# Attention and token mix moved into the second half of each MLP pass, with scores in threes and a new PSUM layout

## Chip, cores and metric

The kernel runs on one core of one Trainium2 chip. The metric is the time of one execution on the device, in microseconds (us); lower is better. Each kernel ran several times, beside the kernel before on the same chip.

## The reference, cut to what matters

Eight batches go through grouped-query attention (16 query heads, 4 key heads, 384 tokens, head size 64) and then through a ResMLP layer of width 1024.

```python
def reference(q, k, v, alpha1, beta1, w_tok, alpha2, beta2, w_ch1, w_ch2, lam):
    x = attention(q, k, v)                     # per batch [384, 1024], softmax over the keys
    a1 = alpha1 * x + beta1
    tok = einsum('ts,bsd->btd', w_tok, a1)     # token mix
    u = x + lam * tok
    a2 = alpha2 * u + beta2
    ch = maximum(a2 @ w_ch1, 0) @ w_ch2        # the MLP: 1024 -> 4096 -> 1024
    return u + lam * ch
```

## The kernel before

It makes eight passes, numbered 0 to 7. Pass b runs the MLP of batch b on TensorE (`main`), and between its matmuls the attention and token mix of batch b+1 (`side`). A pass has two halves. The first computes hT with 256 matmuls of 384 columns (group h) and streams the first weight matrix, 16 blocks of 512 KB, through a ring of five buffers. The second computes the output with 192 matmuls of 512 columns (group ch) from resident weights, so nothing streams then except the first five blocks of the next pass.

```python
RING = 5
def load_w1(n):                                   # one block of the first weights, cast on the way
    t = sb.tile([P, NDT, CW * P], bf, tag="w1", name="w1", bufs=RING)
    nc.gpsimd.dma_start(out=t, in_=w1src[...])
def flip_k(b):                                    # k and q of batch b, transposed by DMA, on SyncE's queue
    nc.sync.dma_start_transpose(out=kT..., in_=k2s[b]...)     # 1,536 packets of 256 B
def flip_q(b):
    nc.sync.dma_start_transpose(out=qT..., in_=qrs[b]...)     # 3,072 packets of 256 B
# ... cut: loads, transposes, constants ...
def main(b):
    for c in range(NCH):                          # first half: 16 blocks of weights
        w1 = w1_tiles.pop(b * NCH + c)
        for j in range(CW):
            ps = psum.tile([P, 512], f32, tag="mm", name="h", bufs=2)
            for dt in range(NDT):
                nc.tensor.matmul(out=ps[:, :n], lhsT=w1[...], rhs=a2T[...], ...)
            # ... relu to hT on ACT or VectorE, in turn ...
        load_w1(b * NCH + c + RING)
    for dw in range(NDW):                         # second half
        for ms in range(NST):
            ...                                   # 32 ch matmuls, two VectorE operations, output store
# the main loop of before: pieces of side() spread evenly over the pass
    for dt in main(b):
        t += dt
        if done < len(us) and done * t_all * span < len(us) * (t - t_all * lead):
            us[done](); done += 1
        if not loaded and t > t_all * 0.55:
            load_next(b + 2)
        if not flipped and t > t_all * (0.85 if b else 0.75):
            flip_k(b + 2); flip_q(b + 2)
```

In `side`, scores come two groups at a time (`scores2`); a group is a PSUM tile of two banks, exponentiated by ACT. Then come av (attention times v; VectorE divides and scales), tok (token mix; VectorE adds and scales) and a2T (transposed by DMA for the next pass).

The softmax here doesn't subtract the row's maximum and nothing guards it: scores larger than these inputs give would overflow.

## Time and profile before

| | before |
|---|---|
| median | 811.8 us (811.3 to 812.1, 3 runs) |
| TensorE busy in the profile | 98% of 808.8 us |
| a steady pass (2 to 6) | 97.45 us |
| its first / second half | 48.85 / 48.6 us |
| last pass, first half, no attention in it | 41.6 us |

A profile line of a group gives source line, engine, operation, output<-inputs, count, then busy time and mean length of one, then the engine's idle time ahead of it and what ended most of it. A timeline line gives start, length, engine and group. The busy time by stretch, here for the two halves of the pass that starts at 331 us, gives for each stretch its length, each engine's busy time with instruction count, the granted clock, the DMA share and GB/s:

```profile
331.00:379.85 48.85, 48.75 (x396) 29.51 (x395) 19.97 (x37) 19.27 (x27) 13.16 (x15) 1.00 1.31 167
379.85:428.44 48.59, 48.11 (x336) 24.58 (x342) 21.29 (x39) 7.04 (x8) 7.90 (x12) 1.00 0.66 108
```

TensorE is full in both halves, and the DMA moves 167 GB/s in the first and 108 in the second. The issues of SyncE's queue show the k and q transposes late in that second half:

```profile
415.50 1.46 SPq L113 DMA_TRANSPOSE kT<-k  x1
417.14 3.94 SPq L117 DMA_TRANSPOSE qT<-q_raw  x1
```

Their issue takes 5.6 us in all.

### The profile page before, as it was taken

Reading aid. Unit: us, or ns where it says so; the run is one execution under the profiler, and the core shown is the slowest. Engines: PE = TensorE matmul, PEld = TensorE weight load, DVE = VectorE, ACT = ScalarE, POOL = GpSimd, SP = SyncE. Lnnn points to the kernel's source line nnn. Section 1 sums busy time; section 2 is a strip of 40 time slices with the busy share of each in tenths; the row PEclk is TensorE's granted clock in tenths of the full one; section 3 lists DMA queues with packets and bytes.
Section 4 is the critical chain, followed back from the end, with each engine's and each line's share of the span. In section 5 each row is a group of like instructions: output and inputs, shape, how many; then the busy total and the mean of one; then the engine's idle time right before and its main releaser. Section 6 shows DMA issues by size and latency. Waiting matters only on the chain.

```text
span 808.8 us, 14107 instructions
## 1 busy us (share of the span) xinstructions
PE 795.7 (98%) x6076; PEld 450.2 (56%) x6129; DVE 343.3 (42%) x669; ACT 226.0 (28%) x311; POOL 178.4 (22%) x232
## 2 busy tenths in 40 slices
PE   8999999999999999999999999999999999999997
PEld 4766554665556645565455654556555565556545
DVE  7645452344433444344452445434444244432122
ACT  6654212332123311233103331034211332102100
POOL 7234320324003230124102250022400320003000
PEclk9999999999999999999999999999999999999999
DMA  9999999999279993799748996499935999129511
GB/s 192 198 207 200 207 197 185 172 178 148 54 139 181 171 133 80 130 178 175 100 113 128 173 180 88 100 154 166 184 60 113 151 171 126 40 66 190 81 40 40
DMA packets 233550, 112.96 MB, mean 140 GB/s; under 512 B 82952, under 2 KB 227344, under 8 KB 233488
## 3 DMA queue, kind: packets, MB, share of 16 engines
q0 software_dynamic: 170736, 83.47, 83.9%
q1 hardware_dynamic: 62208, 28.20, 14.8%
q8 instruction: 48, 0.79, 0.4%
q10 hardware_dynamic: 544, 0.39, 0.2%
q14 instruction: 14, 0.11, 0.0%
HBM read 170.53 MB, written 12.58 MB: 226 GB/s over the span
## 4 chain that ended last, share of the span: by engine, by line
PE 92%; DVE 4%; DMA 3%; issue 1%; ACT 0%; POOL 0%; SPq 0%; DVEq 0%
PE h L413 39%; PE ch L448 38%; PE av L237 4%; PE sc L202 4%; PE tok L259 4%; DMA w<-in_moe_w_ch_dram 2%; DVE x L243 1%; DVE hT L423 1%; PE h L152 1%; DVE a1f L250 0%; DMA a2T<-a 0%; DVE a L252 0%; PE warm L466 0%; PE ut L276 0%; PE tp L188 0%
## 5 line engine op out<-in xcount | busy, mean ns | idle before, releaser
L413 PE MATMUL h<-a2T,w 128*128 128x384 bf16 (+1 forms) x2016 | 349.7, 326 | 1.0 <-DVE hT L423 0.3
L448 PE MATMUL ch<-w,hT 128*128 128x512 bf16 (+2 forms) x1547 | 345.3, 370 | 4.3 <-issue 1.0
L413 PEld LDWEIGHTS <-w 128*128 128x128 bf16 x2016 | 189.4, 98 | 125.8 <-issue 9.0
L448 PEld LDWEIGHTS <-hT 128*128 128x128 bf16 x1600 | 146.3, 98 | 154.2 <-issue 5.8
L128 POOL DMA_DIRECT2D w<-in_moe_w_ch_dram x128 | 112.6, 882 | 540.9 <-PE h L413 502.1
L211 ACT ACTIVATE es<-sc 128x1024 bf16<-128x1024 f32 x126 | 123.4, 1021 | 289.8 <-PE sc L202 289.8
L423 DVE TENSOR_SCALAR hT<-h,bias 128x384 bf16<-128x384 f32 x128 | 79.0, 618 | 187.9 <-PE h L413 187.4
L421 ACT ACTIVATE hT<-h,bias 128x384 bf16<-128x384 f32 x128 | 74.3, 581 | 203.1 <-PE h L413 202.6
L453 DVE TENSOR_TENSOR o<-ch,vecs 128x512 f32<-128x512 f32 (+2 forms) x50 | 33.4, 667 | 91.1 <-PE ch L448 91.1
L266 DVE TENSOR_TENSOR x<-tok,x 128x384 f32<-128x384 f32 x64 | 35.6, 556 | 80.2 <-PE tok L259 78.0
L237 PEld LDWEIGHTS <-es 128*128 128x128 bf16 x1008 | 45.8, 97 | 20.5
L237 PE MATMUL av<-v,es 128*128 128x65 bf16 x1008 | 49.0, 193 | 0.0
L202 PE MATMUL sc<-qT,kT 64*128 64x384 bf16 (+2 forms) x576 | 45.5, 272 | 0.7 <-DMA qT<-q_raw 0.6
L259 PEld LDWEIGHTS <-wtokT 128*128 128x128 bf16 x576 | 37.8, 98 | 13.8 <-DVE x L243 1.6
L242 DVE RECIPROCAL rinv<-av 128x6 f32<-128x6 f32 x64 | 12.4, 193 | 71.2 <-PE av L237 70.9
L259 PE MATMUL tok<-a,wtokT 128*128 128x128 bf16 x504 | 37.3, 219 | 0.0
L243 DVE TENSOR_TENSOR x<-av,rinv 128x384 f32<-128x384 f32 x64 | 35.7, 557 | 2.2
L202 PEld LDWEIGHTS <-kT 64*128 64x128 bf16 x576 | 20.2, 94 | 28.4 <-issue 23.9
L454 DVE TENSOR_TENSOR o<-o,x 128x512 f32<-128x512 f32 (+2 forms) x50 | 33.6, 671 | 1.7
L270 DVE TENSOR_TENSOR a<-x,vecs 128x384 bf16<-128x384 f32 x56 | 31.7, 566 | 1.9
L250 DVE TENSOR_TENSOR a1f<-x,vecs 128x384 f32<-128x384 f32 x56 | 31.5, 562 | 1.9
L252 DVE TENSOR_TENSOR a<-a1f,vecs 128x384 bf16<-128x384 f32 x56 | 31.2, 558 | 2.2
(75 smaller groups left out, 194.7 us busy)
## 6 DMA issues: line engine op xcount, KB each, us to landing
w<-in_moe_w_ch_dram POOLq DMA_DIRECT2D x138, 512.0 KB, 7.8
out_dram<-o SPq DMA_DIRECT2D x47, 256.0 KB, 2.2
q_raw<-in_q_dram POOLq DMA_DIRECT2D x28, 192.0 KB, 7.2
kst<-in_k_dram SPq DMA_DIRECT2D x16, 192.0 KB, 3.2
w<-in_moe_w_ch_dram POOLq DMA_DIRECT2D x1, 2048.0 KB, 16.2
v<-in_v_dram POOLq DMA_DIRECT2D x24, 64.0 KB, 7.0
w<-in_moe_w_ch_dram POOLq DMA_DIRECT2D x4, 256.0 KB, 10.0
a2T<-a SPq DMA_TRANSPOSE x54, 2.3
```

What stands on the lines that cost most here:

```text
L128: nc.gpsimd.dma_start(out=t, in_=w1src[:, :, c * CW * P:(c + 1) * CW * P])
L202: nc.tensor.matmul(out=sc[:, hh, k % 4:k % 4 + n], lhsT=kT[r, sk, 2 * p // G, :], rhs=qT[r, p, st:st + n, :], start=True, stop=True)
L211: nc.scalar.activation(out=e, in_=sc, func=EXP, scale=scale_qk)
L237: nc.tensor.matmul(out=av[:, hh, sq, :], lhsT=ess[k // 4][:, m % 2, k % 4, :], rhs=vb[:, sk, hk, :], start=(sk == 0), stop=(sk == NST - 1))
L243: nc.vector.tensor_tensor(out=x[:, :, cols(p)].rearrange("p st (h d) -> p h st d", h=2), in0=av[:, :, :, :D], in1=rinv.to_broadcast([P, 2, ...
L259: nc.tensor.matmul(out=ps[:, tt, :], lhsT=wtokT[:, st, tt * P:(tt + 1) * P], rhs=a1s[p][:, st, :], start=(st == 0), stop=(st == NST - 1 an ...
L266: nc.vector.tensor_tensor(out=u, in0=ps, in1=u, op=ADD)
L413: nc.tensor.matmul(out=ps[:, :n], lhsT=w1[:, dt, j * P:(j + 1) * P], rhs=a2T[:, dt, :n], start=(dt == 0), stop=(dt == NDT - 1))
L421: nc.scalar.activation(out=hT[:, nt, :], in_=ps[:, :S], func=RELU, bias=c1)
L423: nc.vector.tensor_scalar(out=hT[:, nt, :], in0=ps[:, :S], scalar1=c1, scalar2=0.0, op0=ADD, op1=mybir.AluOpType.max)
L448: nc.tensor.matmul(out=ps[:, lo:hi], lhsT=hT[:, nt, ms * P:(ms + 1) * P], rhs=w2[:, nt, dw * 512 + lo:dw * 512 + hi], start=(nt == 0), sto ...
L454: nc.vector.tensor_tensor(out=o[:, lo:hi], in0=o[:, lo:hi], in1=x[:, ms, c], op=ADD)
```

## The change

The intent: from pass 1 on, attention and token mix run in the second half only, by a fixed table of steps (a step is four ch matmuls, 0.87 us). The first half is then a bare stream of h matmuls. Scores come three groups at a time, so six score blocks a pass instead of nine. This needs six PSUM banks for scores, so when pass 0 is done its PSUM pool is closed and a ring of three double banks, shared by scores, av and tok, is opened. The transposes of k and q move to the start of the next pass.

```diff
+    mms = ST(tc.psum_pool(name="mms", bufs=2))
+    lead_banks = ExitStack()
+    psum = lead_banks.enter_context(tc.psum_pool(name="psum", bufs=2))
+    threes = []
+    def three():
+        return threes[0].tile([P, 2, 4, P], f32, tag="sc", name="sc", bufs=3)
 ... scores, av and tok take three() when b > 1 ...
+        def scores3(i, later=False):
+            for k in range(3):
+                scores(3 * i + k, later and k == 2)
+        if b > 1:
+            return {0: [(scores3, 0)], 4: [(av, 0)], 6: [(scores3, 1)], 8: [(tok_flip, 0)], 11: [(av, 1)],
+                    13: [(scores3, 2, True)], 15: [(av, 2)], 16: [(tok_flip, 1)], 18: [(av, 3)], 19: [(tok_flip, 2)],
+                    20: [(scores3, 3)], 22: [(tok_flip, 3)], 24: [(av, 4)], 27: [(scores3, 4)], 29: [(tok_flip, 4)],
+                    31: [(av, 5)], 33: [(scores3, 5, True)], 35: [(av, 6), (tok_flip, 5)], 37: [(av, 7)],
+                    39: [(tok_flip, 6)], 41: [(tok_flip, 7)]}
 ... the main loop ...
+            if 0 < b < B - 1:
+                flip_k(b + 1)
+                flip_q(b + 1)
             if b + 2 < B:
                 load_k(b + 2)
             for dt in main(b):
                 t += dt
+                if b == 0: ... as before ...; continue
-                if not loaded and t > t_all * 0.55:
+                if not loaded and t > t_all * 0.52:
                     load_next(b + 2)
-                if not flipped and t > t_all * (0.85 if b else 0.75):
-                    flip_k(b + 2)
-                    flip_q(b + 2)
+                if t >= 2 * NNT * T_H:
+                    for f, *a in us.get(u, []):
+                        f(*a)
+                    u += 1
+            if b == 0:
+                lead_banks.close()
+                threes.append(ST(tc.psum_pool(name="threes", bufs=3)))
```

More of the change, by code (lines that the diff above doesn't have):

```diff
@@ L63 @@
     sb = ST(tc.tile_pool(name="sb", bufs=2))
-    psum = ST(tc.psum_pool(name="psum", bufs=2))
+    mms = ST(tc.psum_pool(name="mms", bufs=2))
+    lead_banks = ExitStack()
+    psum = lead_banks.enter_context(tc.psum_pool(name="psum", bufs=2))
+    threes = []
     ident = const.tile([P, P], bf, tag="ident", name="ident")
@@ L133, in load_w2, with bank @@
         nc.gpsimd.dma_start(out=w2[:, r, cs], in_=w2src[:, r, cs])
+    def bank(shape, tag, name, dtype=f32):
+        if tag == "mm":
+            return mms.tile(shape, dtype, tag="mm", name=name, bufs=2)
+        return psum.tile(shape, dtype, tag=tag, name=name, bufs=2 if tag == "sc" else 1)
+    def three():
+        return threes[0].tile([P, 2, 4, P], f32, tag="sc", name="sc", bufs=3)
     def tp_ps(shape, tag="tp"):
-        return psum.tile(shape, bf, tag=tag, name="tp", bufs=2 if tag == "mm" else 1)
+        return bank(shape, tag, "tp", bf)
     late = []
@@ L148, in h_part @@
             if nt % 2 == 0 and nt not in early:
-                t = psum.tile([P, 2, 512], f32, tag="sc", name="h", bufs=2)
+                t = bank([P, 2, 512], "sc", "h")
                 early[nt], early[nt + 1] = t[:, 0], t[:, 1]
@@ L165, in side @@
         first = b == 0
-        pe_flip = b < 2
         def cols(p):
@@ L185, in q_transpose @@
             f = src.dtype == f32
-            ps = psum.tile([P, n * NST, P], src.dtype, tag=tag, name="tp", bufs=2 if tag == "mm" else 1)
+            ps = bank([P, n * NST, P], tag, "tp", src.dtype)
             for i in range(n * NST):
@@ L194, in scores @@
         def scores(i, later=False):
-            sc = psum.tile([P, 2, 4, P], f32, tag="sc", name="sc", bufs=2)
+            sc = bank([P, 2, 4, P], "sc", "sc") if b < 2 else three()
             k = 4 * i
@@ L223, in scores2 @@
             scores(2 * j + 1, True)
+        def scores3(i, later=False):
+            for k in range(3):
+                scores(3 * i + k, later and k == 2)
         def av_piece(p, hh):
-            while late:
+            while late and b < 2:
                 late.pop(0)()
             if hh == 0:
-                avs[p] = psum.tile([P, 2, NST, D1], f32, tag="mm" if first else "av", name="av",
-                                   bufs=2 if first else 1)
+                if b < 2:
+                    avs[p] = bank([P, 2, NST, D1], "mm" if first else "av", "av")
+                else:
+                    avs[p] = three()[:, 0].rearrange("p k s -> p (k s)")[:, :2 * NST * D1].rearrange(
+                        "p (h st d) -> p h st d", h=2, st=NST)
             av = avs[p]
@@ L254, in tok @@
         def tok(p):
-            tag, n = ("mm", 2) if first else ("av", 1) if pe_flip else ("tp", 1)
-            ps = psum.tile([P, NST, P], f32, tag=tag, name="tok", bufs=n)
+            ps = bank([P, NST, P], "mm" if first else "av", "tok") if b < 2 else three()[:, 0, :NST]
             for tt in range(NST):
@@ L273, in a2_transpose @@
             if first:
-                ps = psum.tile([P, NST, P], f32, tag="tp" if p % 2 else "av", name="ut", bufs=1)
+                ps = bank([P, NST, P], "tp" if p % 2 else "av", "ut")
                 for tt in range(NST):
@@ L280, in a2_transpose @@
                 return
-            if not pe_flip or p < 6:
+            if b > 1 or p < 6:
                 nc.sync.dma_start_transpose(
@@ L304, in rows_r @@
         def rows_r(tag):
-            ps = psum.tile([P, 512], f32, tag=tag, name="r", bufs=1)
+            ps = bank([P, 512], tag, "r")
             for st in range(NST):
@@ L321, in spread @@
             n = len(ps_)
-            ps = psum.tile([P, 4, P], f32, tag=tag, name="vec", bufs=1)
+            ps = bank([P, 4, P], tag, "vec")
             w = vs[1] - vs[0]
@@ L333, in add, with av @@
             us.append(lambda: f(*a))
+        def av(p):
+            av_piece(p, 0)
+            av_piece(p, 1)
+            if b > 1:
+                while late:
+                    late.pop(0)()
         def tok_flip(p):
@@ L337, in tok_flip @@
             a2_transpose(p)
-        if not first:
-            if pe_flip:
-                add(split, 2, 4)
-                add(k_transpose, 0)
-                add(q_transpose, 0, 2, "av")
-                add(k_transpose, 2)
-                add(q_transpose, 2, 2, "av")
+        if b > 1:
+            return {0: [(scores3, 0)], 4: [(av, 0)], 6: [(scores3, 1)], 8: [(tok_flip, 0)], 11: [(av, 1)],
[3 more added lines that the diff above has]
+                    39: [(tok_flip, 6)], 41: [(tok_flip, 7)]}
+        if not first:
+            add(split, 2, 4)
+            add(k_transpose, 0)
+            add(q_transpose, 0, 2, "av")
+            add(k_transpose, 2)
+            add(q_transpose, 2, 2, "av")
             for j in range(NP + 4):
@@ L351, in side @@
                     add(scores2, j)
-                    if pe_flip and j in (1, 3):
+                    if j in (1, 3):
                         add(q_transpose, 4 + 2 * (j // 2))
                 if 2 < j < NP + 3:
-                    add(tok if pe_flip else tok_flip, j - 3)
-                if pe_flip and j > 3:
+                    add(tok, j - 3)
+                if j > 3:
                     add(a2_transpose, j - 4)
-                if pe_flip and j < 2:
+                if j < 2:
                     for p in (4 * j, 4 * j + 2):
@@ L361, in side @@
                     add(spread, range(4 * j, 4 * j + 4), (3, 4), "tp", "ACT")
-                elif j < 2:
-                    us.extend([lambda: None] * 2)
             return us
@@ L369, in side @@
         lower, upper = range(NP // 2), range(NP // 2, NP)
-        def av(p):
-            av_piece(p, 0)
-            av_piece(p, 1)
         ut = a2_transpose
@@ L410, in main @@
                 begun = b == 0 and nt in early
-                ps = early[nt] if begun else psum.tile([P, 512], f32, tag="mm", name="h", bufs=2)
+                ps = early[nt] if begun else bank([P, 512], "mm", "h")
                 for dt in range(0 if begun else NDT):
@@ L442, in main @@
             for ms in range(NST):
-                ps = psum.tile([P, 512], f32, tag="mm", name="ch", bufs=2)
+                ps = bank([P, 512], "mm", "ch")
                 o = sb.tile([P, 512], f32, tag="tmp", name="o", bufs=4)
@@ L463, in warmup @@
         def warmup(n):
-            warm = psum.tile([P, 512], f32, tag="mm", name="warm", bufs=2)
+            warm = bank([P, 512], "mm", "warm")
             for _ in range(n):
@@ L563 @@
         for b in range(B):
-            us = side(b + 1) if b + 1 < B else []
+            us = side(b + 1) if b + 1 < B else {}
             half = False
-            done, t, loaded, flipped = 0, 0, b == 0 or b + 2 >= B, b + 2 >= B
-            lead, span = (0.04, 0.82) if b == 0 else (0, 0.95)
+            done, t, u = 0, 0, 0
+            loaded = b == 0 or b + 2 >= B
+            if 0 < b < B - 1:
+                flip_k(b + 1)
+                flip_q(b + 1)
             if b + 2 < B:
@@ L571 @@
                 t += dt
-                half = not half
-                if late and half:
-                    late.pop(0)()
-                if done < len(us) and done * t_all * span < len(us) * (t - t_all * lead):
-                    us[done]()
-                    done += 1
-                if not loaded and t > t_all * 0.55:
+                if b == 0:
+                    half = not half
+                    if late and half:
+                        late.pop(0)()
+                    if done < len(us) and done * t_all * 0.82 < len(us) * (t - t_all * 0.04):
+                        us[done]()
+                        done += 1
+                    continue
+                if not loaded and t > t_all * 0.52:
                     loaded = True
                     load_next(b + 2)
-                if not flipped and t > t_all * (0.85 if b else 0.75):
-                    flipped = True
-                    flip_k(b + 2)
-                    flip_q(b + 2)
-            while done < len(us):
-                us[done]()
-                done += 1
+                if t >= 2 * NNT * T_H:
+                    for f, *a in us.get(u, []):
+                        f(*a)
+                    u += 1
+            if b == 0:
+                assert done == len(us)
+                lead_banks.close()
+                threes.append(ST(tc.psum_pool(name="threes", bufs=3)))
 _INS = ['q', 'k', 'v', 'moe_alpha1', 'moe_beta1', 'moe_w_tok', 'moe_alpha2', 'moe_beta2', 'moe_w_ch1', 'moe_w_ch2', 'moe_lam']
```

## The prediction

> **What bounds the kernel now.** I read the page's first part and its costliest groups first, then the waits of TensorE, then TensorE's order of time through one pass, then the DMA queues.
>
> ```profile
> PE 795.7 (98%) x6076; PEld 450.2 (56%) x6129; DVE 343.3 (42%) x669; ACT 226.0 (28%) x311; POOL 178.4 (22%) x232
> L413 PE MATMUL h<-a2T,w 128*128 128x384 bf16 (+1 forms) x2016 | 349.7, 326 | 1.0 <-DVE hT L423 0.3
> L448 PE MATMUL ch<-w,hT 128*128 128x512 bf16 (+2 forms) x1547 | 345.3, 370 | 4.3 <-issue 1.0
> ```
>
> TensorE is busy for 98%, and the idle time ahead of its two big groups is 1.0 and 4.3 us in the whole run. The waits of TensorE list nothing over 1.5 us. So TensorE's instruction stream is the bound, and only fewer or cheaper TensorE instructions, or their packing, can gain. The chain of waits says the same (PE 92%). Here is that stream inside the steady pass that starts at 331.0 us (start, length, group):
>
> ```profile
> 348.44 2.11 PE L413 MATMUL h<-a2T,w 128*128 128x384 bf16 x12
> 350.49 0.61 PE L202 MATMUL sc<-qT,kT 64*128 64x256 bf16 x8
> 351.03 2.12 PE L413 MATMUL h<-a2T,w 128*128 128x384 bf16 x12
> 352.99 0.43 PE L237 MATMUL av<-v,es 128*128 128x65 bf16 x9
> 353.26 2.11 PE L413 MATMUL h<-a2T,w 128*128 128x384 bf16 x12
> ...
> 360.68 0.67 PE L259 MATMUL tok<-a,wtokT 128*128 128x128 bf16 x9
> 361.19 2.11 PE L413 MATMUL h<-a2T,w 128*128 128x384 bf16 x12
> ```
>
> Starts, not lengths, give costs, as matmuls overlap. Nine av matmuls hold TensorE for 353.26-352.99 = 0.27 us, nine tok for 0.51, two groups of scores (8 matmuls) for 0.54; and the 12 h matmuls ahead of scores take 2.05 where those ahead of av take 1.96, so a score block costs 0.10 more at its entry: 0.64 to 0.65 in all. Passes 1 to 6 start 97.4 to 97.5 us apart (h first at 331.00, 428.44). The last pass, which has no attention, shows the bare MLP half, one group of 256 matmuls:
>
> ```profile
> 720.78 41.76 PE L413 MATMUL h<-a2T,w 128*128 128x384 bf16 x256
> 762.38 38.19 PE L448 MATMUL ch<-w,hT 128*128 128x512 bf16 x188
> ```
>
> That is 41.6 us for the first half (162.5 ns each) and 192 x 0.2164 = 41.5 for the second. Adding 9 x 0.65 + 16 x 0.27 + 8 x 0.505 = 14.2 gives 97.3: the steady pass is explained without any wait. What the change can gain is bounded by that.
>
> The weights matter next. In the last pass the first half streams eleven 512 KB blocks of the first weight matrix through a ring of five; the DMA queues between 728 and 757 us read:
>
> ```profile
> q0 software_dynamic: 10738, 5.41, 140.0%
> w<-in_moe_w_ch_dram POOLq DMA_DIRECT2D x9, 512.0 KB, 7.3
> ```
>
> 10,738 packets in 29 us are 370 per us, so a block (1,024 packets of 512 B) takes 2.77 us, while TensorE uses one in 16 x 0.1625 = 2.60. Landing takes 5.7 us at the start of that half and 7.7 at its end; about 10.1 is allowed (the four blocks ahead, less the issue). A bare first half is thus already at the limit of the DMA, covered only by the ring. In the steady passes of before it lasts 48.85 us, which is ample.
>
> **What the Trainium skill says.**
> - "TensorE: Matmul & The Clock Gate", section Back-to-back issue gap: N/2.4 + 2.5 ns for warm matmuls, so 162.5 ns at 384 columns and 215.8 at 512. The trace agrees (162.5, 216.4).
> - The same page, section Part 3 (The mechanism): matmuls on different row groups overlap. The trace agrees: 2,048 score columns pass in 0.54 us, which at 2.4 per ns would be 0.85 one after the other.
> - "DMA: Bandwidth & Descriptors", section Queues, rings and completion order: each engine round-robins between its queue rows by packet. The trace agrees: where the k and q transposes of the first pass run beside weight loads, between 122 and 131 us, both queues move the same number of packets:
>
> ```profile
> q0 software_dynamic: 2096, 1.06, 87.0%
> q1 hardware_dynamic: 2082, 0.52, 47.5%
> ```
>
> - "PSUM — Partial Sum Buffer", Specifications: 8 banks of 2 KiB. The new layout fills them: two for h and ch, three double banks shared by scores, av and tok. The trace doesn't show banks.
>
> **The change, part by part, for each of passes 1 to 6.**
> 1. Scores in threes. The number of matmuls per kind is the same in both instruction orders. Nine score blocks become six. A block of two holds 1,024 concurrent columns, 0.43 us, so its fixed part is 0.65-0.43 = 0.22; three blocks less save 0.66 us. Joining av's halves saves nothing: nine cost 0.27 wherever they stand.
> 2. Moving attention out of the first half. The matmuls cost the same there as elsewhere, so no gain by itself: the first half falls to 41.6 us, the second rises to 41.5 + 6 x 0.86 + 8 x 0.54 + 8 x 0.505 = 55.
> 3. PSUM in a ring of three double banks. I walked through the second half with the durations of before: exp 1.02 us; after av on VectorE 0.20, then three of 0.56; after tok two of about 0.57; after each ch tile 0.68 and 0.69. Nearly everywhere the buffer is free in time. The exception is the fourth threesome of scores, at step 20: its third group needs the bank of the tok one step before, whose eviction stands behind av 3's four VectorE operations, those behind tok 1's, a ch eviction and av 2's. TensorE should wait 0.7 to 0.9 us there; the after order does give that group a wait on VectorE. I take 0.75.
> 4. The k and q transposes move from 85% of the previous pass, where the DMA is nearly idle, to the start of the first half, where the weights stream. Their 4,608 packets of 256 B (1.2 MB) took the queue 1.46 and 3.94 us to issue alone (at 415.5 us), but 4.06 and 13.24 beside weights (at 115.4). From the shared stretch: 9 us = 2,096 x 2.70 ns + 2,082 x c, so c = 1.60 ns of the whole DMA per transpose packet. They issue about 2.0 us into the half, after the last output store (332.64 in the pass above); weights' packets start at 4.3 to 5. Some 1,400 go ahead for nothing; the other 3,200 cost 5.1 us, and the k load behind them some 0.8. The last block landed 36.6 us into the half in the last pass and is needed at 15 x 2.6 = 39.0. So 36.6 + 5.9 = 42.5, up to 3.5 us late. If the slower stretch at 742 to 747 us in the last pass was chance, 1.5 to 2. I take 2.2.
> 5. The first pass no longer ends with these transposes beside weights and queued ahead of an a2T transpose, which delayed the first h of pass 1 (0.58 idle at 136.58 and gaps near it): about 1 us gained, once.
>
> Sum per pass: -0.66 + 0.75 + 2.2 = +2.3; six passes +13.7; less 1.0: +12.7, so 811.8 becomes about 824.
>
> **The rivals.**
> - *Ring and DMA hold.* If transposes slip through the gaps (the ring starts full, 13 us ahead) and VectorE is a little faster than I walked, only part 1 and 5 remain: 811.8 - 4 - 1 = 807. For it: such a hand-set table of steps looks tuned, and a ring of five hid everything before. Against it: the measured 370 packets per us leave nothing spare in a bare half.
> - *DMA starvation at its full size.* 3.5 to 4 us per pass and PSUM 0.9: +3.9 x 6 - 1 gives 834. For it: the arithmetic without my discount. Against it: once TensorE stalls the ring is exactly full of requests, and the last pass's slow stretch need not recur.
> - *ACT or VectorE becomes the bound of the second half.* VectorE has 8 x 1.9 + 8 x 1.15 + 6 x 1.4 = 33 us there, ACT 18 x 1.02 = 18, both under 55. Local queues only, as in part 3.
> - *A large gain* is ruled out: with no wait in a steady pass, nothing but 0.66 us a pass can come back.
>
> **Range and chances.** The middle is 824. The lower rival is 807, the upper 834; I give 808 to 834 eight chances in ten. The 2% lines are 795.6 and 828.1. Faster than the first needs 2.7 us per pass that aren't there: 0.02. Slower than the second needs a first half over 2.9 us late: about a third. The rest is within 2%.
>
> **What would show it.** Right: first halves of 43 to 45 us with TensorE waits on weight DMA from about the eighth block on, landing times near 10 us, q0 and q1 packets equal early in that half, transposes' issue near 13 us instead of 4; score blocks six a pass at about 0.86 us; one wait of scores on VectorE of about 0.75 us in each second half near its step 20; second halves of about 56 us. Wrong: first halves at 41.6 us with no wait on weights (then 807 to 811); or many waits on exp or VectorE through the second half (part 3 wrong, and above 830); or a lower granted clock after the stalls, which I leave out.

## The result, and the profile after

| | before | after |
|---|---|---|
| median | 811.55 us (811.0 to 812.1, 4 runs) | 849.54 us (848.9 to 850.2, 4 runs) |
| ratio | 1 | 1.0468 (95%: 1.0450 to 1.0486) |
| TensorE busy in the profile | 98% of 808.8 us | 95% of 847.8 us |
| a steady pass (2 to 6) | 97.45 us | 102.5 to 106.1 us |

The change made the kernel slower by 4.7%. A ratio is the mean time of one kernel's runs over that of the other's in the same rounds, so it is not quite the ratio of the medians.

The first part of the page after, and its two big groups:

```profile
PE 806.9 (95%) x6129; PEld 451.0 (53%) x6129; DVE 342.6 (40%) x669; ACT 227.9 (27%) x311; POOL 177.6 (21%) x232
L439 PE MATMUL h<-a2T,w 128*128 128x384 bf16 (+1 forms) x2016 | 344.4, 330 | 29.8 <-DMA w<-in_moe_w_ch_dram 29.4
L474 PE MATMUL ch<-w,hT 128*128 128x512 bf16 (+2 forms) x1600 | 356.5, 371 | 0.9 <-DVE o L479 0.9
```

Idle time ahead of h grew from 1.0 to 29.8 us, and the transfer of w, the weights, ended nearly all of it. The group ch has less idle time than before. So the loss is in the first halves. Stretches of the two halves of the pass that starts at 344.66 us:

```profile
344.66:393.73 49.07, 44.48 (x270) 25.81 (x268) 11.27 (x18) 9.56 (x17) 13.52 (x16) 0.97 1.32 174
393.73:448.47 54.74, 54.35 (x471) 29.08 (x469) 29.78 (x58) 17.07 (x18) 7.49 (x12) 1.00 0.55 89
```

The first half lasts 49.07 us up to the first ch, though only 256 h matmuls (41.6 us bare) and one score block (0.77) are in it. TensorE's timeline of that half:

```profile
344.66 15.76 PE L439 MATMUL h<-a2T,w 128*128 128x384 bf16 x96
362.25 2.77 PE L439 MATMUL h<-a2T,w 128*128 128x384 bf16 x16 [1.83 <-DMA w<-in_moe_w_ch_dram]
367.78 25.25 PE L439 MATMUL h<-a2T,w 128*128 128x384 bf16 x144 [2.75 <-DMA w<-in_moe_w_ch_dram]
392.96 0.83 PE L214 MATMUL sc<-qT,kT 64*128 64x384 bf16 x12
```

After 96 matmuls, which are six blocks, TensorE waits for the seventh block and then longer for the eighth. After the second wait, 144 matmuls take 25.25 us instead of 23.4: from 368.2 us on the granted clock is 0.5 for 3.4 us, and ten or so matmuls start 0.32 us apart, which is half pace (0.97 is the mean of the half). This did not set the end: in each of the six passes the first half of h ended 2.6 to 3.0 us after the last block landed, and a block's own 16 matmuls take 2.6.

The issues of SyncE's queue, and the DMA queues of the same half in five stretches (352 to 355 us, 350 to 352, 355.5 to 357.5, 363 to 364, 372 to 388):

```profile
346.74 1.36 SPq L118 DMA_TRANSPOSE kT<-k  x1
348.28 8.91 SPq L122 DMA_TRANSPOSE qT<-q_raw  x1
```
```profile
q0 software_dynamic: 708, 0.36, 88.1%
q1 hardware_dynamic: 704, 0.18, 46.3%
```
```profile
DMA packets 391, 0.17 MB, mean 86 GB/s; under 512 B 91, under 2 KB 391, under 8 KB 391
```
```profile
DMA packets 490, 0.18 MB, mean 90 GB/s; under 512 B 279, under 2 KB 490, under 8 KB 490
```
```profile
DMA packets 34, 0.01 MB, mean 12 GB/s; under 512 B 20, under 2 KB 34, under 8 KB 34
```
```profile
q0 software_dynamic: 6268, 3.16, 145.4%
```

q0 carries the weights and q1 the transposes. Issuing the q transpose took 8.91 us instead of 3.94. While both run, each queue moves 235 packets per us; alone the weights move 392 (the last line, 6,268 in 16 us). There are also slow stretches: 391 packets in the 2 us in which the first weight packets arrive among the transposes, 490 in 2 us at 355.5 (about half the shared pace), and 34 in the microsecond after an instruction fetch. The first of them is in part the weights' own: without any transposes, in the last pass of before, they also move only 421 packets in their first 2 us (725.3 to 727.3).

By the issues and landings of the weights in the trace, the last block lands 44.3 to 47.8 us into the six first halves. It is needed at 39.0.

### The profile page after: what moved, and what is told of

It is laid out like the page before. It is cut to its first block, busy times and chain, and to the rows that moved or that the text cites. A ratio compares the mean times of both kernels' runs of the same rounds, so it can differ in the third digit from the quotient of the medians.

```text
span 847.8 us, 14176 instructions
## 1 busy us (share of the span) xinstructions
PE 806.9 (95%) x6129; PEld 451.0 (53%) x6129; DVE 342.6 (40%) x669; ACT 227.9 (27%) x311; POOL 177.6 (21%) x232
## 4 chain that ended last, share of the span: by engine, by line
issue 44%; DMA 25%; PE 23%; POOL 5%; DVE 3%; POOLq 0%; ACT 0%; DVEq 0%
DMA w<-in_moe_w_ch_dram 25%; PE ch L474 9%; PE h L439 8%; POOL w L133 5%; PE sc L214 1%; PE h L165 1%; PE av L257 1%; PE tok L278 1%; PE sc L257 0%; DVE x L263 0%; PE ut L295 0%; PE warm L492 0%; PE sc L278 0%; PE tp L200 0%; DVE hT L561 0%
## 5 line engine op out<-in xcount | busy, mean ns | idle before, releaser
L439 PE MATMUL h<-a2T,w 128*128 128x384 bf16 (+1 forms) x2016 | 344.4, 330 | 29.8 <-DMA w<-in_moe_w_ch_dram 29.4
L474 PE MATMUL ch<-w,hT 128*128 128x512 bf16 (+2 forms) x1600 | 356.5, 371 | 0.9 <-DVE o L479 0.9
L439 PEld LDWEIGHTS <-w 128*128 128x128 bf16 x2016 | 194.4, 99 | 171.5 <-DMA w<-in_moe_w_ch_dram 42.9
L257 PEld LDWEIGHTS <-es 128*128 128x128 bf16 x1008 | 39.3, 97 | 14.3
L214 PE MATMUL sc<-qT,kT 64*128 64x384 bf16 (+2 forms) x576 | 43.5, 272 | 2.4 <-DVE x L285 2.3
L278 PEld LDWEIGHTS <-wtokT 128*128 128x128 bf16 x576 | 37.4, 98 | 13.8 <-DVE x L263 1.7
L285 DVE TENSOR_TENSOR x<-sc,x 128x384 f32<-128x384 f32 x48 | 26.5, 552 | 31.5 <-PE sc L278 31.0
L262 DVE RECIPROCAL rinv<-sc 128x6 f32<-128x6 f32 x48 | 9.2, 192 | 66.1 <-PE sc L257 66.1
L257 PE MATMUL sc<-v,es 128*128 128x65 bf16 x864 | 34.1, 193 | 0.0
L278 PE MATMUL sc<-a,wtokT 128*128 128x128 bf16 x432 | 31.9, 219 | 0.0
L263 DVE TENSOR_TENSOR x<-sc,rinv 128x384 f32<-128x384 f32 x48 | 26.7, 557 | 1.6
```

Of the source, the lines that this page charges most:

```text
L214: nc.tensor.matmul(out=sc[:, hh, k % 4:k % 4 + n], lhsT=kT[r, sk, 2 * p // G, :], rhs=qT[r, p, st:st + n, :], start=True, stop=True)
L257: nc.tensor.matmul(out=av[:, hh, sq, :], lhsT=ess[k // 4][:, m % 2, k % 4, :], rhs=vb[:, sk, hk, :], start=(sk == 0), stop=(sk == NST - 1))
L278: nc.tensor.matmul(out=ps[:, tt, :], lhsT=wtokT[:, st, tt * P:(tt + 1) * P], rhs=a1s[p][:, st, :], start=(st == 0), stop=(st == NST - 1 an ...
L439: nc.tensor.matmul(out=ps[:, :n], lhsT=w1[:, dt, j * P:(j + 1) * P], rhs=a2T[:, dt, :n], start=(dt == 0), stop=(dt == NDT - 1))
L474: nc.tensor.matmul(out=ps[:, lo:hi], lhsT=hT[:, nt, ms * P:(ms + 1) * P], rhs=w2[:, nt, dw * 512 + lo:dw * 512 + hi], start=(nt == 0), sto ...
```

## The experiments

A common measure is the stretch from the first h to the first ch, for passes 1 to 6, beyond 42.46 us. That is its length where TensorE waits for nothing. Last columns: that excess, summed over six passes, and where the transposes are.

| kernel | median us | ratio to before | excess, us | k and q transposes |
|---|---|---|---|---|
| after | 849.5 | 1.0468 | 40.4 | start of the first half |
| late_flip | 812.5 | 1.0003 | 4.1 | late in the second half |
| k_start_q_late | 809.2 | 0.9966 | 1.4 | k at the start, q late |
| q_start_k_late | 815.9 | 1.0056 | 8.0 | q at the start, k late |
| q_first | 839.4 | 1.0329 | 29.7 | start, q ahead of k |
| hoisted | 817.2 | 1.0051 | 8.5 | 5.5 us earlier in passes 2 to 6 |
| kload_after_store | 842.2 | 1.0381 | 33.4 | start; k load elsewhere |
| ring6 | 834.9 | 1.0279 | 27.0 | start; ring of six |
| before_dummy | 828.2 | 1.0204 | (other halves) | dummies in the kernel before |
| best | 804.8 | 0.9921 | 0 | late |

Two more, kload_late and best_singles, are told below. Every kernel gave the right result. My theory was that the transposes collide with the weights of a bare first half; the rivals stand in the expectations.

### late_flip: undo one part

```diff
-            if 0 < b < B - 1:
-                flip_k(b + 1)
-                flip_q(b + 1)
 ... condensed: the run has these lines twice, for pass 0 and for the others ...
+                if not flipped and t > t_all * (0.85 if b else 0.75):
+                    flipped = True
+                    flip_k(b + 2)
+                    flip_q(b + 2)
```

> The changed kernel with only the k and q transposes put back where the kernel before has them (85% of the previous pass, where the weights don't stream). Theory A (the transposes collide with the weight stream of the bare first half): the 41 us of waits on weights in six passes vanish, first halves 41.6 to 42.5 us, second halves as in the changed kernel (55.5 us with the scores ahead of the first ch), so passes of about 97.1 us and 806 to 811 us in all. Rival B (the bare first half outruns the weight stream whatever else the DMA does): first halves stay at 46 us or more, over 835 us.

It took 812.5 us, ratio 1.0003 (0.9967 to 1.0038). Passes 2 to 6 did as expected: first halves 42.46, second 54.74, so 97.2 us, with no wait on weights. The total missed the range by 1.5 us. The waits of TensorE show why:

```profile
PE h L439 <- DMA a2T<-a: 2.6, 1, 2.6
```

The 4.1 us are all in pass 1: in pass 0 the q transpose runs beside weight loads, and an a2T transpose that pass 1 needs stands behind it on SyncE's queue. Rival B falls: a bare first half keeps pace with the weights, and its last block lands at 36.8 to 38.2 us in passes 2 to 6. So moving the transposes is the cause of the loss.

### k_start_q_late and q_start_k_late: one transpose each

Either `flip_k(b + 1)` or `flip_q(b + 1)` goes back to the start of the pass; the other stays late.

> As late_flip, but the k transpose (a third of the packets) stays at the start of the first half; only the q transpose is late. Theory A, by packets in time: the k packets are through in about 2 us, before the first weight packets, so nearly no wait on weights: within 3 us of late_flip. Rival C (any transpose near the start of the stream upsets it, for example by stopping both queues where they meet): 1 us or more of waits on weights in each pass, 6 us or more above late_flip.

> The complement of k_start_q_late: q's 3,072 packets at the start of the first half, k's 1,536 late. Theory A with packets counted by time: some 1,400 of q's go ahead of the weights, the other 1,700 share (2.7 us) and the stop where the streams meet costs some 1.4, so the last blocks land 4 us later than in late_flip against a slack of 1.3: 2 to 4 us of waits in a pass, 822 to 835 us. Rival C (a stop at the meeting and instruction fetches make the stall, whatever the number of packets): 5 us or more a pass, over 840.

With k at the start: 809.2 us, no excess in passes 2 to 6, and last blocks at 38.4 to 38.8 there. That it is 3.3 us below late_flip comes mostly from pass 1, which loses 1.4 instead of 4.1. With q at the start: 815.9 us, below the expected range, with 0 to 2.3 us of excess a pass. Its issue line points to the reason:

```profile
336.74 3.89 SPq L122 DMA_TRANSPOSE qT<-q_raw  x1
```

3.89 us is the time without company. Between 338 and 342 us, 2,770 packets passed on the transposes' queue and 2 on the weights'. I had counted on 1,400 going ahead and 1,700 sharing. The weights did not start of themselves that late: their first load was issued 3.1 us into the half as ever, but its first packet came at 7.4 us, about when the transpose's last ones went, against 4.8 in late_flip and 5.5 in the changed kernel, where k's 1,536 packets go first. So the transpose ran alone and held the weights up for 2.6 us; why is not shown. Rival C falls: one transpose that is through before the weights' first packets costs little. The excess of the two alone adds up to under 10 us; together, in the changed kernel, they cost 40.

### q_first: the same work in the other order

```diff
-                flip_k(b + 1)
                 flip_q(b + 1)
+                flip_k(b + 1)
```

> The changed kernel with the q transpose issued ahead of the k transpose. In q_start_k_late all 3,072 packets of q were through before the weights got going, while in the changed kernel q's came after k's and had to share. If sharing packet by packet (and the stops that come with it) is what costs, only k's 1,536 packets share now: 2 us less wait in a pass, 833 to 841 us. If the volume alone counts: unchanged, 847 to 851.

839.4 us, within the expected range, with 1.8 us less excess a pass. The same packets cost less when only k's 1,536 of them meet the weights. Issue lines:

```profile
342.65 3.87 SPq L122 DMA_TRANSPOSE qT<-q_raw  x1
346.62 5.37 SPq L118 DMA_TRANSPOSE kT<-k  x1
```

Whichever transpose is second shares, and a longer second one costs more. The first is not free: in pass 4 the weights' packets are 2.4 us behind those of late_flip before k begins to share, and 6.1 behind at the end.

### hoisted: the same work 5.5 us earlier

```diff
-            if 0 < b < B - 1:
+            if b == 1:
 ... cut ...
+                    if u == 45 and b + 2 < B:
+                        flip_k(b + 2)
+                        flip_q(b + 2)
```

> The changed kernel with the k and q transposes of passes 2 to 6 issued about 5.5 us earlier, four steps before the end of the previous second half (pass 1 keeps them at its start). Same work on the same queue, only no longer beside the weights. Theory A: passes 2 to 6 lose all their waits (32 to 33 us), pass 1 keeps its 8: 815 to 819 us. Rival (the transposes' volume near the first half uses up the DMA): half of it stays, 830 or more.

817.2 us, as expected. Passes 2 to 6 have 42.46 to 42.71 us; pass 1, which kept its place, has 50.68. The waits on weights that are left, mostly in pass 1:

```profile
PE h L439 <- DMA w<-in_moe_w_ch_dram: 5.8, 5, 2.8
```

Nothing but a few microseconds' overlap in time separates 49 us halves from 42.5 us ones.

### kload_late and kload_after_store: the k load behind the transposes

> The changed kernel with only the load of k for the pass after next moved from behind the transposes to the start of the second half. The k load took 3 us beside weights at half their rate, about 1.5 us of the stream. Theory A, all transfers add up: 1.5 us less wait in each of five passes, 840 to 844 us. If the transposes alone make the stall: unchanged at 849.

The edit put `load_k` later in the program, and this did nothing: SyncE's queue waits for nothing between the transposes and the first output store of the second half, so it issued the load just after the transposes, as the changed kernel does (first line, kload_late; 847.8 us). The run says nothing on the question. In the second attempt the load stands behind that store (second line). Both edits also put `load_next`, the loads of q and v for the pass after next, later in the second half.

```profile
357.35 1.12 SPq L95 DMA_DIRECT2D kst<-in_k_dram  x2
```
```profile
403.61 1.09 SPq L95 DMA_DIRECT2D kst<-in_k_dram  x2
```

> What kload_late was to be. Its edit changed nothing on the queue of SyncE, which had nothing to wait for and issued the load where it did before; here the load stands behind the first output store of the second half. Theory A, all transfers add up: the k load's 1.5 us beside weights vanish from five passes: 840 to 844 us. Rival: the transposes alone make the stall, 848 to 851.

842.2 us, by the median: 7.0 us less excess in all, 5.3 of it in the five passes that have the load (1.1 a pass). Pass 6, which has no k load in either kernel, differs by the other 1.7, and that is the scatter. 1.1 a pass is not beyond it, so the run suggests that other traffic beside the weights adds up too, and does not show it.

### ring6: one more block of slack

```diff
-    RING = 5
+    RING = 6
```

Room for it came from two buffers instead of four for the outputs and a1f.

> The changed kernel with a ring of six weight blocks instead of five; room comes from two buffers instead of four for the outputs and a1f. Theory A: one more block is 2.6 us more slack, so 2.6 us less wait in each of six passes, 832 to 836 us. Rival E (the DMA can't sustain a bare half once anything is added, ring or not): 845 us or more.

834.9 us, as expected; 2.2 us less excess a pass, where a block is worth 2.6. The transposes delay the stream by a fixed amount, and the ring covers a part of it.

### before_dummy: the collision in the kernel before

Twelve dummy transposes of the same packets, at the start of passes 1 to 6 of the kernel before, write an a2T buffer that is dead at that time.

> The kernel before, with dummy transposes of the same 4,608 packets added at the start of each of passes 1 to 6, where the changed kernel has its transposes; they write a buffer that is dead there, and the result stays right. Its first half lasts 48.9 us, as attention runs in it. Theory A (the collision hurts because the first half is bare and needs a block in 2.60 us): the ring has about 3.05 us for a block and takes up the 8 us that the transposes cost the stream: 0 to 1.5 us of waits in a pass, 812 to 821 us. Rival D (transposes beside weights cost TensorE the same wherever they are): about 41 us more, 850 us.

828.2 us: more than I expected, less than half of rival D. First halves grew by 0.9 to 5.1 us, 2.7 in the mean, and the waits name the weights:

```profile
PE h L413 <- DMA w<-in_moe_w_ch_dram: 11.5, 10, 2.1
```

So the collision costs even where the first half lasts 48.85 us, but 2.7 us a pass instead of 6.7. My expectation looked at the slack of the last block only. The fifth streamed block landed at 28.7 us in pass 2 instead of 20.9, some 8 us late, and the blocks in the middle have less slack than that.

### best, and best_singles: what the rest of the change is worth

```diff
  late_flip, and:
-                    if not flipped and t > t_all * 0.75:      # pass 0
+                    if not flipped and t > t_all * 0.9:
-                    20: [(scores3, 3)], 22: ...
+                    21: [(scores3, 3)], 22: ...
```

> late_flip with two more edits: the transposes of batch 2 at 90% of the first pass instead of 75%, behind that pass's last a2T transpose on the queue of SyncE, and the fourth threesome of scores at step 21 instead of 20. Theory: late_flip lost 4 us at the start of pass 1 to an a2T transpose queued behind the q transpose, and 0.39 us a pass to the wait of scores on VectorE; without both its steady pass of 97.2 us becomes 96.8, so 806 to 808.5 us, a ratio to before of 0.993 to 0.997. Rival: batch 2's transposes now collide with the weights of pass 1 in another place, and 3 us or more are lost there: 810 us or more.

804.8 us, ratio 0.9921 (0.9907 to 0.9936): faster than both kernels, though by under 1% than before, and a little better than expected. The first half is one group again, and the halves are:

```profile
329.36 41.76 PE L439 MATMUL h<-a2T,w 128*128 128x384 bf16 x256
```
```profile
329.36:371.82 42.46, 42.46 (x270) 25.42 (x268) 11.27 (x18) 9.55 (x17) 13.53 (x16) 1.00 1.29 181
371.82:426.01 54.19, 53.41 (x462) 29.09 (x470) 29.81 (x58) 17.07 (x18) 7.48 (x12) 1.00 0.63 106
```

A steady pass takes 96.65 us against 97.45 of the kernel before.

best_singles cuts the six threesomes of best into eighteen single groups, with ch matmuls between them.

> best with its six threesomes of scores a pass cut into eighteen single groups, ch matmuls between them (k and q transposes two steps later, behind the last group). It measures the fixed cost of a score block by itself: twelve blocks more by 0.21 to 0.22 us are 2.6 us a pass, 15 to 16 us in six: 820 to 821 us. If the threes gain by something else (fewer waits on the exponentials, say), the second half grows by another amount than 2.6 us.

822.6 us, 1.6 above the expected range. The second half takes 57.17 us where best takes 54.19, and the score block ahead of it is shorter by about two groups, so the pass grew by about the expected 2.6 us (99.3 where no a2T wait was added; up to 0.6 us of such a wait stood in three passes, as the transposes were two steps later). A score block has a fixed cost of about 0.22 us, and this is what the threes gain.

## Why the prediction was wrong

**The mechanism was right, the size was not.** "Slower because the transposes share the DMA with the weights of a bare first half" holds by late_flip, hoisted and q_first. The time lay outside the range, because one term of the sum was mis-sized: step 4, "I take 2.2" us of wait a pass. It measured 6.7 (40.4 over six). With that term the sum closes: 40.4, less 1.5 for six passes of 97.20 instead of 97.45, less 0.9 at the start of pass 1, is 38.0, and 38.0 was measured.

Step 4 failed in two places:

- *"So 36.6 + 5.9 = 42.5"*: the last block landed at 44.3 to 47.8. In passes 2 to 6 that is 6.2 to 10.1 us later than in the same pass of late_flip, which has the k load but not the transposes. Their own cost was put at 5.1. The free packets were counted about right (k's 1,536 went ahead), and q's 3,072 beside weights are 4.9 us by the step's own 1.60 ns. What it left out is that the weights start later (5.5 us into the half, not 4.3 to 5) and that the DMA slows at times: where the streams meet, a few microseconds later at about half the shared pace (490 packets in 2 us), and most after an instruction fetch among transposes beside weights. In five of the six passes such a fetch is followed by 1.3 to 3.6 us with under half the packets of the shared stretch. Pass 4 has no such fetch, and its last block is still 6.2 us late, so the stops after fetches can explain what lies above this, and not the bulk. The step's own source, the stretch between 122 and 131 us, began just after two such stops in the first pass of before, at 105 and 121 us.
- *"If the slower stretch at 742 to 747 us in the last pass was chance, 1.5 to 2. I take 2.2."* This cut the arithmetic's own 3.5. The 36.6 was not made late by chance: the last block of the last pass, which has no transposes in any kernel, landed at 36.8 to 37.7 us in all twelve traces with a ring of five. The cut made the forecast worse, but 3.5 would have given 832, still 17 us short.

The other terms of step 4 held. The k load was put at 0.8 us: in late_flip the last block lands at 37.4 to 38.2 in passes 2 to 5, and at 36.8 in pass 6, which has no such load. And the need at 39.0 fits: the blocks landed 5.3 to 8.8 us after it, and the excess is 5.3 to 8.9 us a pass. Of the signs named, the waits came at the seventh and eighth block, but the issue of the q transpose took 8.9 us and not near 13.

By its other steps:

1. *Scores in threes save 0.66 us a pass.* Right. The block takes 0.86, as computed. Without waits the whole steady pass falls by 0.80 (best), and best_singles gives the fixed cost back.
2. *Moving attention gains nothing by itself; second half 55 us.* Right: 54.74 and the score block ahead of it, 55.5, with the wait of step 3 in it.
3. *One wait of the fourth threesome of scores on VectorE, 0.75 us.* Right in place, half in size. Timeline and waits after:

```profile
417.52 0.39 PE L214 MATMUL sc<-qT,kT 64*128 64x128 bf16 x4 [0.39 <-DVE x L285]
```
```profile
PE sc L214 <- DVE x L285: 2.3, 6, 0.4
```

   One step later it is gone (best).
5. *One microsecond gained once at pass 1.* Its start in the kernel before is 0.93 us longer than that of other passes. In best this is gone; after, it is buried under the stall.

Of the rivals, "DMA starvation at its full size" was the nearest, at 834, and still too small for the reasons above. "Ring and DMA hold" is what late_flip and best show once the transposes are elsewhere. VectorE and ACT didn't become bounds: 29.8 and 17.1 us busy in a second half of 54.7. The lower clock that was left out did come, for 3.4 us in each of four of the six passes, after single waits of 2.7 to 2.9 us, and cost next to nothing.

**What is open.** Why the DMA slows after an instruction fetch among transposes and weights, where the streams meet, and once more between. Most fetches that fall among transposes and weights are followed by a stop (in after at 105.0, 142.0, 254.7, 362.8, 557.0 and 671.2 us), and most fetches beside weights alone are not. But one in after, at 674.5 us, is not either: 239 packets of transposes and 247 of weights pass in the microsecond behind it. No run took the fetches away, so that they are the cause is not shown. How much of the 6.2 to 10.1 us each kind of slow stretch makes is not separated.

## What to carry to other kernels

When work is moved out of a stage to make it shorter, compare the supply rate of that stage with its new pace before looking at instruction costs: here a block of weights needed 2.6 us of DMA in a stage that then used one every 2.6 us, and anything put beside it turned into waiting. Move transfers that can go elsewhere to a time when the queue is empty, and look at the queue, not at the program's order, for when they are issued. Take a cost under contention from several stretches, with the stops in it, and don't cut an arithmetic that the profile supports on the guess that a slow stretch was chance.

## What the Trainium skill lacked or had wrong

- "DMA: Bandwidth & Descriptors", section Queues, rings and completion order: the round-robin by packet fits where both streams run (708 and 704 packets in 3 us), but it gives no cost: weights fall from 392 packets of 512 B per us to 236 beside 256 B transpose packets. Nor does it say that a stream issued behind a running transpose starts late: 2 packets against 2,770 in 4 us in q_start_k_late.
- The same page, Rules for kernel authors, says that "a transpose next to ordinary DMAs needs nothing". The row is about correctness, and the results here were right. It says nothing of time: 40 us in 850.
- No page has the slow stretches of the DMA: 490 packets in 2 us where 940 would pass at the shared pace, 34 in the microsecond after an instruction fetch.
- "TensorEngine Tiling (Array Packing)", section Key Properties, says that changing the tiling mode drains TensorE, without a figure; here a block of 64-row scores among 128-row matmuls has a fixed cost of about 0.22 us (that the drain makes it is not shown).
